# v of a linear-attention kernel: loaded six tokens per partition, cast on GpSimd, and turned twice by TensorE

## The chip, the cores and the metric

The kernel runs on one core of a Trainium2 chip. The metric is the device time of one execution in microseconds (us); less is better. Engines are named as in the profile: PE is TensorE's matmul, PEld its weight load, DVE is VectorE, ACT is ScalarE, POOL is GpSimd and SP is SyncE. "L233" is line 233 of the kernel before.

## The reference

Two stages follow each other. The first is a linear attention (RWKV-5) with B = 4, H = 8, S = 768 tokens and D = 48: a state of 48 x 48 per head decays by w and takes in one outer product per token.

```python
for t in range(S):
    kt, vt, rt = (k[:, :, t], v[:, :, t], r[:, :, t])
    cur = np.einsum('bhd,bhe->bhde', u[None] * kt, vt)
    y[:, :, t] = np.einsum('bhd,bhde->bhe', rt, state + cur)
    state = w[None, :, :, None] * state + np.einsum('bhd,bhe->bhde', kt, vt)
```

The second is a soft mixture of experts on x, which is y laid out as 3072 tokens of 384 numbers: logits = x @ phi with 32 slots (8 experts of 4 slots), a softmax over the tokens gives each slot its input, each expert is a pair of matrices (384 x 1024, relu, 1024 x 384), and a softmax over the slots mixes the slots' outputs back into the tokens. The weights w1 and w2 are 25 MB of float32 in HBM.

## The kernel before

**Tiling.** The recurrence is computed in chunks of 128 tokens. A unit m is one batch and one pair of heads (16 units, four to a batch); it has two halves of 384 tokens, three chunks each. The main loop has a step i for each of the 32 halves, from -5 on so that the pipeline fills; `mu, odd = divmod(i, 2)` gives the unit. In a step, the work of several units stands side by side: the products of unit mu + 3 (odd steps: k) and mu + 2 (even steps: r), the turns of unit mu + 2, the scores of half i + 1, the output of half i. Every instruction goes through `O(...)`, which keeps it in the order in which it is written, engine by engine. So each engine has a fixed queue, and an instruction that waits holds up all that is behind it on its engine.

**k and r.** They are loaded with six tokens to a partition (`load_kr`, L116): partition p holds tokens 6p to 6p + 5 of a head, 1152 bytes in one piece. `scale` (L228) multiplies them by powers of w and casts to bf16, on POOL for all units but the first; the factors W come from DVE (`tt`) and an exponential on ACT (`ex`), which are spread over the first steps. `t_pe` (L236) turns them on PE with six transposes, and `t_evac` (L242) copies the result out of PSUM on ACT in an order that puts token 6s + j at column 6s + j. For k, `b_pe` and `b_evac` (L249 to L257) turn that once more, to have it with the tokens of a chunk on the partitions. There are three buffers for `scale`'s result, so the product of unit m waits for the turns of unit m - 3.

**v.** It is loaded with three tokens to a partition for each half (`load_v`, L120), 576 bytes in one piece. `v_cast` (L267) makes it bf16: on POOL for unit 0, on ACT for all others, at the end of the even steps. `v_pe` (L283) puts a half in the order of tokens with nine matmuls, each of which picks a third of a chunk's tokens with a shifted selection matrix Q3, and `v_evac` (L292) copies the three chunks from the bank Vb on ACT. Each is called once in a step, for half i + 2.

**The weights and the raw buffers.** k, r and v of a batch go to one of three raw buffers; batch 3 goes to the buffer of batch 0, and its loads are issued on SP at step 3. The weights are loaded by POOL, which casts them to bf16 on the way (`load_w`, L138): w1 into a tile of its own, w2 into the raw buffers of batches 1 and 2. Their place in POOL's queue is given by a table, from step 12 on; ahead of the first stands `guard` (L576), a copy of one column of k of batch 3, which makes POOL wait until that has landed. The table's numbers are how many loads a step issues:

```python
W_AT = {12: 1, 13: 1, 14: 1, 15: 1, 17: 1, 19: 1, 20: 1, 22: 1, 23: 1, 25: 1, 26: 5}
```

**After the loop** come the last logits, then the experts: the first matrices (L628), relu, transposes (L653), the second matrices (L665, in tiles of 32 columns, one for each of four experts), and the output: a scaled matmul (L689) for each 128 tokens, and eight stores.

Of the kernel before, what the change touches and what calls it, by code (L numbers as in the profile page):

```python
# [9 lines left out]
def kernel(  # L10
# [13 lines left out]
    B, H, S, D = r.shape  # L24
    C = 128
    nC = S // C
# [7 lines left out]
    nQ = H // 2  # L34
    G = 2
    L = nC // G
    T = L * C
    P2 = 2 * D
    nN = Nn // C
    nG = B * G  # L40
    nU = B * nQ
    nH = nU * G
    J = S // C
    JV = T // C

    f32 = mybir.dt.float32
    bf = mybir.dt.bfloat16
# [4 lines left out]
    def O(ins):  # L52
        return tc.keep_in_program_order(ins)

    pe, dve, act, pool, sp = nc.tensor, nc.vector, nc.scalar, nc.gpsimd, nc.sync
# [3 lines left out]
    wk = ctx.enter_context(tc.tile_pool(name="wk", bufs=3))  # L59
# [14 lines left out]
    def raw_of(which, b):  # L74
        return raw[b % NR][:, which * RW:(which + 1) * RW]
# [3 lines left out]
    Ab = psb.tile([128, 2, 512], f32, name="Ab")  # L79
# [3 lines left out]
    Vb = psb.tile([128, 512], f32, name="Vb")  # L83
# [25 lines left out]
    O(act.dma_start(out=wu3[0:4, :, 0:D], in_=w.rearrange("(q e) d -> q e d", e=2)))  # L109
    O(act.dma_start(out=wu3[4:8, :, 0:D], in_=u.rearrange("(q e) d -> q e d", e=2)))  # L110
    O(dve.memset(warm, 0.0))
    O(dve.memset(one_f, 1.0))
    zt = cst.tile([128, nQ, 3, P2], f32, name="zt")
    O(dve.memset(zt[:], 0.0))

    def load_kr(which, src, b, h0, h1):  # L116
        O(sp.dma_start(out=raw_of(which, b).rearrange("p (h x) -> p h x", h=H)[:, h0:h1, :],
                       in_=src[b, h0:h1].rearrange("h (p j) d -> p h (j d)", j=J)))

    def load_v(b, h0, h1):  # L120
        O(sp.dma_start(out=raw_of(2, b).rearrange("p (h x) -> p h x", h=H * G)[:, h0 * G:h1 * G, :],
                       in_=v[b, h0:h1].rearrange("h (g p j) d -> p (h g) (j d)", g=G, j=JV)))

    def load_batch(b, step, h=0):
        for h0 in range(h, H, step):
# [32 lines left out]
    Q3 = cst.tile([128, QW], bf, name="Q3")  # L158
# [17 lines left out]
    ident = cst.tile([128, 128], bf, name="ident")  # L176
# [4 lines left out]
    def spread(bank, a, z):  # L181
        O(pe.matmul(bank[:, 0:z - a], one_f, w_row[:, a:z], start=True, stop=True))
        O(act.activation(out=lnw[:, a:z], in_=bank[:, 0:z - a], func=AF.Ln))
# [7 lines left out]
    def tt(j, q):  # L191
        e = (sk, sr)[j]
        O(dve.tensor_mul(W[j][:, q], lnw[:, None, q * P2:(q + 1) * P2].to_broadcast([128, J, P2]),  # L193
                         e[:, :, None].to_broadcast([128, J, P2])))

    def ex(j, q):
        O(act.activation(out=W[j][:, q], in_=W[j][:, q], func=AF.Exp))

    tt(0, 0)
    tt(1, 0)  # L200
    spread(Vb, P2, H * D)
    ex(0, 0)
    ex(1, 0)
    wT = cst.tile([128, nQ], f32, name="wT")
# [20 lines left out]
    st = {}  # L225
# [31 lines left out]
        O(dve.tensor_copy(kn[:].rearrange("p c t -> p (c t)"), T0[:, 0:S]))  # L257

    def prod_f(m):
        pr = wk.tile([128, S], bf, name="prod", bufs=2)  # L260
        st["prod", m] = pr
        O(dve.tensor_mul(pr[:].rearrange("p (s j) -> p s j", j=J),  # L262
                         T1[:, 0:S].rearrange("p (j s) -> p s j", j=J),
                         st["kT", m][:].rearrange("p (s j) -> p s j", j=J)))


    def v_cast(m):  # L267
        b, q = divmod(m, nQ)
        vb = wk.tile([128, 2, G, JV, D], bf, name="v_bf", bufs=2)
        st["vb", m] = vb  # L270
        out, src = vb[:].rearrange("p h g j d -> p (h g j d)"), raw_of(2, b)[:, 2 * q * G * JV * D:2 * (q + 1) * G * JV * D]
        if m == 0:
            O(pool.tensor_copy(out, src))
        else:
            O(act.copy(out, src))  # L275


    def at(i):
        m, g = divmod(i, G)
        b, q = divmod(m, nQ)  # L280
        return m, b, q, g, b * G + g

    def v_pe(i):  # L283
        m, b, q, g, n = at(i)
        vb = st["vb", m]
        for c in range(L):
            for j in range(JV):
                o = C * c - j + JV - 1
                O(pe.matmul(Vb[:, c * P2:(c + 1) * P2], Q3[:, o:o + C], vb[:, :, g, j, :],  # L289
                            start=(j == 0), stop=(j == JV - 1)))  # L290

    def v_evac(i):  # L292
        vn = wk.tile([128, L, 2, D], bf, name="vn", bufs=3)
        st["v", i] = vn
        O(act.copy(vn[:].rearrange("p c e d -> p (c e d)"), Vb[:, 0:L * P2]))  # L295

    def a_pe(i):
        m, b, q, g, n = at(i)
        kT, rT = st["kT", m], st["rT", m]
        for c in range(L):  # L300
            t = slice((g * L + c) * C, (g * L + c + 1) * C)
            for e in range(2):
                s = slice(64 * e, 64 * e + 64)
                O(pe.matmul(Ab[:, e, c * C:(c + 1) * C], kT[s, t], rT[s, t]))  # L304

    def mask_f(i):
        AT = wk.tile([128, 2, L, C], bf, name="AT", bufs=2)
        st["AT", i] = AT
        O(dve.tensor_mul(AT[:], Ab[:, :, 0:T].rearrange("p e (c t) -> p e c t", c=L),  # L309
                         mask_ut[:, None, None, :].to_broadcast([128, 2, L, C])))  # L310
# [123 lines left out]
    def disp_ev(n, ds_p):  # L434
        if n == 0:
            O(dve.tensor_copy(acc[:], ds_p))
        else:
            O(dve.tensor_add(acc[:], acc[:], ds_p))
# [60 lines left out]
    for i in range(-5, nH):  # L499
        mu, odd = divmod(i, 2)  # L500
        if 0 <= i + 1 < nH:
            a_pe(i + 1)
            mask_f(i + 1)
        if pend:
            disp_ev(*pend.pop())
        if i == nH - 1:
            turn(n0, (2,), Vb[:].bitcast(bf), act)
            disp(n0 - 1, ds_t)
            le_t(n0 - 1)
            let_ev(n0 - 1, None, dve)  # L510
        if 0 <= i < nH:
            y_pe(i)
            y_evac(i)
        if 0 <= i + 2 < nH:
            v_pe(i + 2)
            v_evac(i + 2)
        if 0 <= i + 1 < nH:
            m_pe(i + 1)
            z_evac(i + 1)
        if odd == 0 and 0 <= mu + 1 < nU:  # L520
            prod_f(mu + 1)
        if odd and i > 0 and mu + 2 < nU:
            b_pe(mu + 2)
            b_evac(mu + 2)
        if odd and 0 <= mu + 3 < nU:
            scale(mu + 3, 0)
        if not odd and 0 <= mu + 2 < nU:
            scale(mu + 2, 1)
        route(i, 0)
        if 0 <= mu + 2 < nU:  # L530
            t_pe(mu + 2, odd)
            route(i, 1)
            t_evac(mu + 2, odd)
            if odd and i < 0:
                b_pe(mu + 2)
                b_evac(mu + 2)
        else:
            route(i, 1)
        if odd == 0 and 0 <= mu + 2 < nU:
            v_cast(mu + 2)  # L540
        route(i, 2)
        if i == nH - 3:
            turn(n0, (0, 1), T0, act)
        if i == nH - 2:
            turn(n1, (0, 1), T1, act)
        for f, j, q in T_AT.get(i, ()):
            f(j, q)
        if i in (-4, -3):
            wu_steps(i + 4)
        if i in Z_AT:  # L550
            q = Z_AT[i]
            O(act.activation(out=zt[:, q, 2, :], in_=zt[:, q, 0, :], func=AF.Copy, scale=wT[:, q:q + 1]))
        if i == 2:
            O(pool.memset(ones[:], 1.0))
            for t in Le_t:
                O(pool.memset(t[:], 0.0))
        if i == 3:
            load_kr(0, k, B - 1, 0, H)
            load_kr(1, r, B - 1, 0, H)
            for h0 in range(0, H, 2):  # L560
                load_v(B - 1, h0, h0 + 2)
        if i == 5:
            O(act.copy(phi_b, phi_f))
        if i == 6:
            for mi in range(nM):
                for j in range(nM):
                    o = C * mi - j + nM - 1
                    O(pe.matmul(Xb[:, mi * ES:(mi + 1) * ES].rearrange("p (j g s) -> p j g s", g=2, s=Spe),
                                Q3[:, o:o + C],
                                phi_b[:, j * ES:(j + 1) * ES].rearrange("p (g j s) -> p j g s", g=2, s=Spe),  # L570
                                start=(j == 0), stop=(j == nM - 1)))
            O(act.copy(phi_s[:].rearrange("p m s -> p (m s)"), Xb[:, 0:nM * ES]))
        if i == 28:
            O(pool.memset(uns, 0.0))
        if i == min(W_AT):
            O(pool.tensor_copy(guard[:], raw_of(0, B - 1)[:, 0:1]))  # L576
        for _ in range(W_AT.get(i, 0)):
            load_w(nw)
            nw += 1
# [44 lines left out]
    for g in range(2):  # L624
        for a in range(2):
            for mi in range(nM):
                for j in range(EG):
                    O(pe.matmul(hb[g][a][32 * j:32 * j + 32, 0:FH], uns[:, mi, g, j, :],  # L628
                                w1_all[:, g * EG + j, mi, a * FH:(a + 1) * FH],
                                start=(mi == 0), stop=(mi == nM - 1), skip_group_check=True))  # L630
            src = hb[g][a][:, 0:FH].rearrange("p (q y) -> p y q", y=nF)
# [63 lines left out]
    i = 0  # L695
# [44 lines left out]
```

The softmax here doesn't subtract the row's maximum and nothing guards it: scores larger than these inputs give would overflow.

## Time and profile before

The time before is 121.42 us, the median of three runs (121.41 to 121.73). The profiled execution spans 119.7 us.

| engine | busy us | share of the span | instructions |
|---|---|---|---|
| PE | 101.7 | 85% | 1797 |
| DVE | 95.0 | 79% | 187 |
| ACT | 83.7 | 70% | 183 |
| POOL | 58.9 | 49% | 70 |

Instructions that the change touches, or that are near to those it brings:

| line, engine, what | count | mean ns of one |
|---|---|---|
| L233 POOL product of k or r | 30 | 1417 |
| L273 POOL cast of v (unit 0) | 1 | 667 |
| L275 ACT cast of v (other units) | 15 | 679 |
| L289 PE matmuls of v | 288 | 208 |
| L295 ACT copy of a half's v | 32 | 418 |
| L240 PE transposes of k and r | 192 | 225 |
| L246 ACT copy of kT, rT | 32 | 801, 804 |

The span is cut into 40 slices, and the rows of digits give each engine's busy share in tenths; one slice is 3 us. The shares are means over stages with different limits: an attention loop until about 87 us, the experts' matrices until about 103 us, the stores after it. A matmul's mean duration contains its passage through the array; what a row of matmuls costs is read from the distance between the starts of two rows in the timeline. The same goes for DVE and ACT, where an instruction begins some 0.1 us before the one ahead of it is recorded as done. In the timeline, a bracket after an instruction is the time that its engine was idle ahead of it, and what ended that. In the DMA rows, q0 is the queue of POOL's transfers and q1 that of SP's.

### The profile page before, as it was taken

The page shows a single profiled execution, that of the slowest core. Times are in us where ns is not written, and L with a number is a line of the kernel's source. Part 1 is how long each engine was busy: PE and PEld are TensorE (multiplying, and loading weights), DVE is VectorE, ACT ScalarE, POOL GpSimd, SP SyncE. Part 2 cuts the span into 40 slices and gives each one's busy share as a digit, 9 for nine tenths or more (in the row PEclk, how much of TensorE's full clock was granted, in tenths as well). Part 3 has the DMA queues.
Part 4 walks back from the last instruction along what each step waited for, and adds up shares of the span by engine and source line. Part 5 has one row for each costly group of instructions (what it writes and reads, how often), then busy time and mean ns, then how long its engine had stood idle before and what let it go on. Part 6 is the DMA issues. An engine that isn't in the chain of part 4 may idle for free.

```text
span 119.7 us, 4336 instructions
## 1 busy us (share of the span) xinstructions
PE 101.7 (85%) x1797; PEld 81.9 (68%) x1797; DVE 95.0 (79%) x187; ACT 83.7 (70%) x183; POOL 58.9 (49%) x70
## 2 busy tenths in 40 slices
PE   5897877799999999999999999999979996795000
PEld 1456766578988888898888888888866686682000
DVE  6889999999999999899999899999943510499000
ACT  4259987898979988888898988998964510398000
POOL 7326744699999999796877591111000000011100
PEclk9999999999999999999999999999999999999855
DMA  3999999999999999999999999999999997179991
GB/s 89 365 344 372 377 370 370 333 393 358 320 384 381 342 219 224 211 220 207 223 207 225 207 218 214 214 215 218 215 216 211 218 203 146 17 288 386 427 407 70
DMA packets 20797, 31.79 MB, mean 266 GB/s; under 512 B 1129, under 2 KB 17898, under 8 KB 20650
## 3 DMA queue, kind: packets, MB, share of 16 engines
q0 software_dynamic: 2960, 15.34, 57.1%
q1 hardware_dynamic: 17648, 16.03, 39.7%
q8 instruction: 14, 0.23, 0.7%
q10 hardware_dynamic: 170, 0.15, 0.4%
q14 instruction: 5, 0.04, 0.1%
HBM read 39.38 MB, written 4.72 MB: 368 GB/s over the span
## 4 chain that ended last, share of the span: by engine, by line
PE 39%; DMA 23%; DVE 20%; ACT 6%; issue 4%; POOLq 0%; DVEq 0%; ACTq 0%
DMA raw<-in_moe_w_dram 21%; PE Vb L289 5%; PE T L240 5%; PE Ab L304 4%; PE Yb L357 4%; DVE prod L262 3%; DVE W L193 3%; DVE AT L309 3%; PE Mb L330 3%; PE T L252 3%; DVE raw L691 2%; PE Yb L370 2%; DMA LexpT<-in_w_dram 2%; ACT rT L246 2%; PE Xb L392 2%
## 5 line engine op out<-in xcount | busy, mean ns | idle before, releaser
L233 POOL TENSOR_TENSOR kr<-raw,W 128x576 bf16<-128x576 f32 x30 | 42.0, 1417 | 13.6 <-PE T L240 5.1
L309 DVE TENSOR_TENSOR AT<-Ab,mask_ut 128x768 bf16<-128x768 f32 x32 | 30.4, 949 | 0.8 <-PE Ab L304 0.6
L289 PE MATMUL Vb<-v_bf,Q 128*128 128x96 bf16 x288 | 17.8, 208 | 0.3 <-ACT vn L295 0.3
L289 PEld LDWEIGHTS <-Q 128*128 128x128 bf16 x288 | 16.1, 99 | 1.7 <-issue 0.3
L240 PE MATMUL T<-ident,kr 128*128 128x128 bf16 x192 | 16.6, 225 | 0.7 <-POOL kr L233 0.7
L246 ACT COPY kT<-T 128x768 bf16<-128x768 bf16 x16 | 12.8, 801 | 4.4 <-PE T L240 3.2
L246 ACT COPY rT<-T 128x768 bf16<-128x768 bf16 x16 | 12.9, 804 | 3.4 <-PE T L240 2.8
L262 DVE TENSOR_TENSOR prod<-T,kT 128x768 bf16<-128x768 bf16 x16 | 15.2, 950 | 0.0
L347 DVE TENSOR_TENSOR dv<-vn,Mb 128x288 bf16<-128x288 bf16 x32 | 14.2, 443 | 0.0
L295 ACT CAST vn<-Vb 128x288 bf16<-128x288 f32 x32 | 13.4, 418 | 0.1
L346 DVE TENSOR_TENSOR Z<-Mb,zt 128x288 bf16<-128x288 f32 (+1 forms) x32 | 12.8, 400 | 0.7
L240 PEld LDWEIGHTS <-kr 128*128 128x128 bf16 x192 | 12.2, 100 | 1.5 <-POOL kr L233 0.8
L377 ACT CAST x<-Yb 128x288 bf16<-128x288 f32 x32 | 13.1, 409 | 0.1
L709 POOL DMA_DIRECT2D out_dram<-W x1 | 0.6, 552 | 24.7 <-DVE W L691 24.7
L304 PE MATMUL Ab<-rT,kT 64*128 64x128 bf16 x192 | 10.9, 219 | 2.0 <-DVE AT L309 2.0
L330 PE MATMUL Mb<-vn,kn 128*128 128x96 bf16 (+2 forms) x80 | 11.2, 238 | 0.0
L357 PE MATMUL Yb<-vn,AT 128*128 128x48 bf16 x192 | 10.3, 185 | 0.1
L275 ACT CAST v_bf<-raw 128x576 bf16<-128x576 f32 x15 | 10.2, 679 | 0.0
L143 POOL DMA_DIRECT2D raw<-in_moe_w_dram x10 | 5.5, 558 | 7.9 <-DMA raw<-in_moe_w_dram 2.9
L357 PEld LDWEIGHTS <-AT 128*128 128x128 bf16 x192 | 7.1, 96 | 3.3
L304 PEld LDWEIGHTS <-kT 64*128 64x128 bf16 x192 | 5.5, 94 | 5.5 <-DVE AT L309 1.9
L370 PE MATMUL Yb<-dv,ident 128*128 128x288 bf16 x32 | 9.1, 284 | 0.2
(143 smaller groups left out, 220.2 us busy)
## 6 DMA issues: line engine op xcount, KB each, us to landing
w_all<-in_moe_w_dram POOLq DMA_DIRECT2D x8, 768.0 KB, 13.6
raw<-in_moe_w_dram POOLq DMA_DIRECT2D x7, 768.0 KB, 18.9
raw<-in_v_dram SPq DMA_DIRECT2D x12, 288.0 KB, 7.2
raw<-in_r_dram SPq DMA_DIRECT2D x8, 288.0 KB, 5.2
raw<-in_k_dram SPq DMA_DIRECT2D x2, 1152.0 KB, 9.9
raw<-in_r_dram SPq DMA_DIRECT2D x2, 1152.0 KB, 9.3
raw<-in_k_dram SPq DMA_DIRECT2D x7, 288.0 KB, 6.0
out_dram<-raw POOLq DMA_DIRECT2D x1, 1536.0 KB, 6.7
```

The source lines that it names most:

```text
L233: O(eng.tensor_mul(kr[:, j].rearrange("p j (h s) -> p j h s", s=64)[:, :, :, 0:D], src, W[j][:, q].rearrange("p j (h d) -> p j h d", h=2)))
L240: O(pe.transpose(bank[:, x * C:(x + 1) * C], kr[:, j, x, :], ident[:]))
L246: O(act.copy(t[:].rearrange("p (s j) -> p s j", j=J), bank[:, 0:S].rearrange("p (j s) -> p s j", j=J)))
L262: O(dve.tensor_mul(pr[:].rearrange("p (s j) -> p s j", j=J), T1[:, 0:S].rearrange("p (j s) -> p s j", j=J), st["kT", m][:].rearrange("p (s ...
L289: O(pe.matmul(Vb[:, c * P2:(c + 1) * P2], Q3[:, o:o + C], vb[:, :, g, j, :], start=(j == 0), stop=(j == JV - 1)))
L295: O(act.copy(vn[:].rearrange("p c e d -> p (c e d)"), Vb[:, 0:L * P2]))
L304: O(pe.matmul(Ab[:, e, c * C:(c + 1) * C], kT[s, t], rT[s, t]))
L309: O(dve.tensor_mul(AT[:], Ab[:, :, 0:T].rearrange("p e (c t) -> p e c t", c=L), mask_ut[:, None, None, :].to_broadcast([128, 2, L, C])))
L330: O(pe.matmul(o, kn[:, g * L + c, :], vc, start=first, stop=True, skip_group_check=True))
L347: O(dve.tensor_mul(dv[:], st["v", i][:].rearrange("p c e d -> p (c e) d"), Mb[:, 288:288 + 2 * L, None].to_broadcast([128, L * 2, D])))
L357: O(pe.matmul(Yb[:, o:o + D], AT[:, e, c, :], vn[:, c, e, :], start=first, stop=False, skip_group_check=True))
L377: O(act.copy(st["x", n][:, :, q * P2:(q + 1) * P2], Yb[:, 0:L * P2].rearrange("p (c e) -> p c e", c=L)))
```

## The change

v is loaded like k and r, six tokens to a partition and 1152 bytes in one piece. Its cast goes to POOL for all units but 1 to 3, which ACT casts, and stands at the end of the odd steps, for unit mu + 3. Selection by matmul is replaced by two turns, a whole unit at a time. At the even steps `vt_pe` turns the two heads of unit mu + 2 with twelve transposes into the partitions 0 to 47 and 64 to 111 of bank Vb, and `vt_evac` copies them out in the order of tokens. At the odd steps `vn_pe` turns the six chunks back, into the same bank, and `vn_evac` copies them out on ACT. The purpose is that one layout and one load function serve all three inputs, and that v is read from HBM in longer pieces. Rows 48 to 63 of Vb are never written by a turn but are read, so the bank is cleared once at the start. The first logarithm's second matmul moves to another bank; `prod`, `v_bf` and `vT` have one buffer each.

```diff
+    O(dve.memset(Vb[:], 0.0))
...
     def load_v(b, h0, h1):
-        O(sp.dma_start(out=raw_of(2, b).rearrange("p (h x) -> p h x", h=H * G)[:, h0 * G:h1 * G, :],
-                       in_=v[b, h0:h1].rearrange("h (g p j) d -> p (h g) (j d)", g=G, j=JV)))
+        load_kr(2, v, b, h0, h1)
...
-    spread(Vb, P2, H * D)
+    spread(Ab[:, 0, :], P2, H * D)
...
-        pr = wk.tile([128, S], bf, name="prod", bufs=2)
+        pr = wk.tile([128, S], bf, name="prod", bufs=1)
...
     def v_cast(m):
-        vb = wk.tile([128, 2, G, JV, D], bf, name="v_bf", bufs=2)
+        vb = wk.tile([128, 2, J, D], bf, name="v_bf", bufs=1)
...
-        if m == 0:
-            O(pool.tensor_copy(out, src))
-        else:
-            O(act.copy(out, src))
+        if 0 < m < nQ:
+            O(act.copy(out, src))
+        else:
+            O(pool.tensor_copy(out, src))
+
+    def vt_pe(m):
+        vb = st["vb", m]
+        for j in range(J):
+            for e in range(2):
+                O(pe.transpose(Vh[64 * e:64 * e + D, j * C:(j + 1) * C], vb[:, e, j, :], ident[:]))
+
+    def vt_evac(m):
+        vT = wk.tile([128, S], bf, name="vT", bufs=1)
+        st["vT", m] = vT
+        O(act.copy(vT[0:PV].rearrange("p (s j) -> p s j", j=J),
+                   Vh[0:PV, 0:S].rearrange("p (j s) -> p s j", j=J)))
+
+    def vn_pe(m):
+        vT = st["vT", m]
+        for c in range(nC):
+            O(pe.transpose(Vh[:, c * C:c * C + PV], vT[0:PV, c * C:(c + 1) * C], ident[0:PV, 0:PV]))
+
+    def vn_evac(m):
+        vn = wk.tile([128, nC, 2, D], bf, name="vn", bufs=3)
...
+        O(act.copy(vn[:].rearrange("p c e d -> p (c e) d"),
+                   Vh[:, 0:S].rearrange("p (x s) -> p x s", s=64)[:, :, 0:D]))
...
-        if 0 <= i + 2 < nH:
-            v_pe(i + 2)
-            v_evac(i + 2)
+        if 0 <= mu + 2 < nU:
+            if odd:
+                vn_pe(mu + 2)
+                vn_evac(mu + 2)
+            else:
+                vt_pe(mu + 2)
+                vt_evac(mu + 2)
...
-        if odd == 0 and 0 <= mu + 2 < nU:
-            v_cast(mu + 2)
+        if odd and 0 <= mu + 3 < nU:
+            v_cast(mu + 3)
```

More of the change, by code (lines that the diff above doesn't have):

```diff
@@ L264, in prod_f @@
                          st["kT", m][:].rearrange("p (s j) -> p s j", j=J)))
+    Vh = Vb[:].bitcast(bf)
+    PV = 64 + D
     def v_cast(m):
         b, q = divmod(m, nQ)
-        vb = wk.tile([128, 2, G, JV, D], bf, name="v_bf", bufs=2)
+        vb = wk.tile([128, 2, J, D], bf, name="v_bf", bufs=1)
         st["vb", m] = vb
-        out, src = vb[:].rearrange("p h g j d -> p (h g j d)"), raw_of(2, b)[:, 2 * q * G * JV * D:2 * (q + 1) * G * JV * D]
-        if m == 0:
+        out, src = vb[:].rearrange("p h j d -> p (h j d)"), raw_of(2, b)[:, 2 * q * J * D:2 * (q + 1) * J * D]
+        if 0 < m < nQ:
+            O(act.copy(out, src))
+        else:
             O(pool.tensor_copy(out, src))
-        else:
-            O(act.copy(out, src))
+    def vt_pe(m):
[14 more added lines that the diff above has]
+        vn = wk.tile([128, nC, 2, D], bf, name="vn", bufs=3)
+        for g in range(G):
+            st["v", m * G + g] = vn[:, g * L:(g + 1) * L]
+        O(act.copy(vn[:].rearrange("p c e d -> p (c e) d"),
+                   Vh[:, 0:S].rearrange("p (x s) -> p x s", s=64)[:, :, 0:D]))
     def at(i):
@@ L281, in at @@
         return m, b, q, g, b * G + g
[L283 to L295, printed above, removed]
     def a_pe(i):
```

## The prediction

> **What bounds the kernel now.** I read the page first, then the chain and the waits, then the timeline of POOL, then the DMA queues in stretches of 1 us.
>
> ```profile
> DMA  3999999999999999999999999999999997179991
> ...
> DMA raw<-in_moe_w_dram 21%; PE Vb L289 5%; PE T L240 5%; PE Ab L304 4%; PE Yb L357 4%; DVE prod L262 3%; DVE W L193 3%; DVE AT L309 3%; PE Mb L330 3%; PE T L252 3%; DVE raw L691 2%; PE Yb L370 2%; DMA LexpT<-in_w_dram 2%; ACT rT L246 2%; PE Xb L392 2%
> ...
> ACT W L677 <- PE Yb L665: 7.3, 1, 7.3
> PE Xb L665 <- DMA raw<-in_moe_w_dram: 1.5, 3, 0.5
> ```
>
> The DMA engines are full in every slice but the first until slice 33 (about 99 us), and the chain holds one long piece that is no engine's: the weights, from 77.77 to 102.52 us. The second matmuls (L665) stop for their last pieces (at 99.26, 101.15, 102.52), while ACT has had nothing to do for 7.3 us. So the end is the end of the weight transfer at 102.5 us, plus a tail of 119.7 - 102.5 = 17.2 us that the change doesn't touch. The attention loop ends near 87 us, and PE has done all that needs no late weights at 98.7: it has about 0.6 us to spare before the first of these waits. The weight stream runs at a constant 215 GB/s from 42 us on, so it ends early or late as it starts early or late. Who starts it? POOL, in program order:
>
> ```profile
> 22.06 1.42 POOL L233 TENSOR_TENSOR kr<-raw,W 128x576 bf16<-128x576 f32 x1 [1.41 <-ACT W L197]
> 23.41 0.21 POOL L554 MEMSET ones<- 128x128 bf16 x1
> 23.55 0.79 POOL L556 MEMSET Le<- 128x384 bf16 x2
> 24.30 13.72 POOL L233 TENSOR_TENSOR kr<-raw,W 128x576 bf16<-128x576 f32 x10
> 37.95 0.20 POOL L576 COPY guard<-raw 128x1 f32<-128x1 f32 x1
> 38.07 0.75 POOL L140 DMA_DIRECT2D w_all<-in_moe_w_dram  x1
> ```
>
> From 24.30 to the guard there is no bracket: ten products back to back (1.37 us from one start to the next), no wait. POOL is the bound of this stretch, though the page gives it 49% of the span. The DMA queues show what hangs on it (share of 16 engines in the microseconds from 36, 39, 40 and 41):
>
> ```profile
> q1 hardware_dynamic: 344, 0.39, 109.1%
> ...
> q1 hardware_dynamic: 605, 0.34, 108.6%
> ...
> q0 software_dynamic: 1, 0.01, 3.0%
> ...
> q0 software_dynamic: 21, 0.13, 62.1%
> q1 hardware_dynamic: 330, 0.18, 59.6%
> ```
>
> q1 carries r, k, v, q0 the weights. The first weight packet moves just before 41 us, 2.9 us after its issue at 38.07, and q1 runs dry near 41.6. The hand-over is just in time: counting the share that q0 had already, the weights start in effect at 41.3 and need 61.2 us. Any lateness of POOL there is a hole in the DMA.
>
> **What the Trainium skill says.** "GPSIMD Engine Reference", 4.1 Engine selection: elementwise work with one input runs near line rate on GpSimd, with two about twice as slow as VectorE. The trace agrees on the ratio: its one cast (L273) took 0.67 us, a product of the same 576 columns 1.42. "DMA: Bandwidth & Descriptors", Why small descriptors are slow: a fixed cost per packet; the trace shows 0.34 MB/us for v alone (576-byte packets, from 39 us) and 0.39 for k and r (1152 bytes, from 36 us). The same page, Latency and other measured facts, gives about 1 us to the first byte of a GpSimd transfer; here 2.9 us pass, and I use those. "TensorEngine Tiling (Array Packing)", Key Properties: tiles of the array work at the same time, but a change of mode drains it. The trace has the first half: at L665 four tiles of 32 columns with 192 moving columns each take 0.09 us together.
>
> **The change part by part.**
>
> *DMA of v.* v is 4.72 MB. At 0.34 MB/us it takes 13.9 us, at 0.39 12.1. The gain is 1.5 to 1.8 us; q1 would run dry near 40.0.
>
> *POOL.* Casts 4 to 15 move from ACT to POOL. In the queue the casts of units 4, 5, 6, 7 and 8 (steps 3, 5, 7, 9, 11) stand between the memsets and the guard. Each takes 0.67 us, 0.62 as one of a row: 5 x 0.62 = 3.1 us, and there is no idle time to take them in. Behind them stand the guard, all weight issues and the later products. A cast also waits now for vt_pe of the unit before, since v_bf has one buffer. For unit 8 that is PE's step 10, which has its v work at 38.7 us before; POOL reaches this cast, by its own pace alone, about 40.5, so the wait is short or none. Afterwards POOL needs 2 x 1.37 + 0.62 + 0.6 for each issue, 4.0 to 4.6 us a unit, against PE's 4.4: the next weights come in time, the second with little to spare.
>
> *ACT.* A unit had two vn casts (418 ns) and a v cast (679), 1.52 us. It gets a vT copy (as kT, L246: 801) and a vn copy of 576 columns (between the 384-column copy of xT, 0.48, and 801: 0.64), 1.44. From unit 4 on nothing changes. At the start it does: by the last exponential that POOL's products wait for (step 1, run at 21.30), ACT had four vn casts and two v casts; now it has three vT copies, three vn copies and three v casts. From start to start (0.29, 0.58; 0.70, 0.55, 0.58) that is 5.5 us instead of 2.3, 3.2 more. ACT's idle time between 8 and 22 us is 3.1 us, but much of it is waiting for DVE, which itself has almost none from 12 us on:
>
> ```profile
> 18.48 0.69 ACT L197 ACTIVATE W<-W 128x576 f32<-128x576 f32 x1 [0.22 <-DVE W L193]
> 21.30 0.68 ACT L197 ACTIVATE W<-W 128x576 f32<-128x576 f32 x1 [0.84 <-DVE W L193]
> ```
>
> The added work comes ahead of kT, rT and the exponentials in ACT's queue, kT delays kn on DVE, and DVE's next W product delays the next exponential. PE adds to it: vt_pe of unit 0 stands ahead of the first t_pe, when six transposes still take 0.75 us. So the startup slips by something between 0.3 us (all of it in gaps) and 3.2 (none). I take 1.8: following the queues step by step puts kT of unit 1 later by about 2 us, and I hold part of that back. POOL's product at 22.06 waits for exactly this exponential, so its row of products starts 1.8 us later.
>
> *PE.* Before, a unit had 18 matmuls of 96 columns in 2 x 0.38 us. Now it has 12 turns with 48 columns of weights and 128 moving, and 6 of 112. One at a time they cost what t_pe does (0.34 us for six): 0.68 + 0.33 = 1.01 us, 0.25 more. Two at a time in tiles 64 wide: 0.34 + 0.33, 0.09 less. DVE needs 4.4 us a unit in any case, so a saving is worth nothing. I take half, +0.1 us a unit, 1.5 us by the loop's end; with the startup it ends some 3 us later, and PE is ready for the late weights near 102.
>
> *Edits at nothing.* The memset of Vb (about 0.5 us on DVE by the 1.02 us of zt, 2.25 times its size) goes into the 0.55 us in which DVE waits for the first logarithm. One buffer for prod and vT: their next writers come after their last readers have been waited for by the same engine. The logarithm's spread uses another bank.
>
> *Sum.* The first weight is issued 1.8 + 3.1 = 4.9 us later, at 43.0; its first packet moves at 45.9; the DMA is empty from 40.0 to then, so v's shorter transfer buys nothing. The weights end 61.2 us later, at 107.1, against 102.5: +4.6. PE's 102 lies below that. The time is 121.4 + 4.6 = 126.0.
>
> **The rivals.**
> 1. *Only the casts count* (startup slip 0.3, casts 3.1): the weights start 3.4 us later, less the 0.35 us of overlap lost anyway: 121.4 + 3.05 = 124.5. For it: ACT's 3.1 us of gaps. Against: they lie elsewhere than the added work.
> 2. *The transfer decides* and POOL keeps its date: 1.5 us less of DMA, 119.9, faster. For it: the DMA row at 9 throughout and the gap between 0.34 and 0.39. Against: the stretch from 24.30 to 37.95 without a wait.
> 3. *The compute loop becomes the bound*: turns one at a time, drains between tile modes, and the two hops over ACT (vT, then vn in the same bank) that PE waits for with everything queued behind, 0.2 to 0.3 us a step over 32 steps, 6 to 9 us: 128.5 to 131. For it: PE at 9 in the slices and ACT at 2.76 of 3. Against: ACT has a step of about 2.2 us for each hop.
> 4. *No change*: slip and gain cancel, 121.4. Nothing in the profile sets them equal.
>
> **How the numbers follow.** The forecast with slips of 1 to 3 us has 0.70, rival 1 0.12, rival 2 0.06, rival 3 0.10, rival 4 0.02. Faster 0.06, same 0.03, slower 0.91. The bounds of the startup (0.3 to 3.2) give 124.5 to 127.4; a cast cheaper or a first packet sooner takes off 0.7, and weights that come late once or twice add about 1. The range is 123.7 to 128.6, which leaves out rivals 2 and 4 and most of 3.
>
> **What would show it.** Right: the GB/s row has a hole of 5 to 6 us between about 40 and 46 us where before it had none; POOL shows guard and first weight near 43 with five casts in an unbroken row ahead of them; the weights still take 61 us; the end moves with them. The startup slip is read from the start of POOL's row of products (24.30 before). Wrong: the first weight before 41 us (rival 1 or 2); PE waiting for ACT vT or vn in each step, or L665 with no wait for weights (rival 3); a DMA row with no hole. What I see least well is the startup.

## The result, and the profile after

The changed kernel takes 128.12 us (median of four runs, 127.91 to 128.35), the kernel before 121.52 in the same session. The ratio is 1.054, 95% interval 1.052 to 1.057: 6.6 us slower. The forecast was 126.0 (123.7 to 128.6), slower.

The page of the changed kernel, slices of 3.2 us (digits are tenths; GB/s is what the DMA moved), and its chain:

```profile
PEclk9999657999999999999999999999999997699955
DMA  4999999999999008999999999999999999259991
GB/s 110 332 279 362 388 390 381 388 391 386 387 391 320 20 5 158 217 217 208 213 218 213 214 217 210 217 215 224 208 210 219 212 214 194 40 194 382 410 434 74
...
DMA raw<-in_moe_w_dram 19%; DVE AT L322 10%; DVE prod L262 6%; DVE dv L360 5%; POOL kr L233 4%; DVE kn L257 3%; POOL raw L143 2%; PE Xb L682 2%; PE Yb L682 2%; DVE Z L359 1%; PE Vb L284 1%; POOL v_bf L278 1%; PE T L706 1%; PE T L240 1%; PE T L252 1%
```

Where the DMA row held 9 throughout, it now has two zeros, about 41 to 47.5 us. After the hole the weights move at 215 GB/s as before. The chain ends in the weights again, and POOL, absent from it before, is now part of it (its pieces there lie between 73.9 and 82.0 us, at the last issues, not at the guard).

POOL's queue in the changed kernel, the columns being start, duration, instruction and, in brackets, idle time before it:

```profile
25.86 1.41 POOL L233 TENSOR_TENSOR kr<-raw,W 128x576 bf16<-128x576 f32 x1 [1.41 <-ACT W L197]
...
28.09 1.41 POOL L233 TENSOR_TENSOR kr<-raw,W 128x576 bf16<-128x576 f32 x1
29.44 0.67 POOL L278 CAST v_bf<-raw 128x576 bf16<-128x576 f32 x1
30.06 2.78 POOL L233 TENSOR_TENSOR kr<-raw,W 128x576 bf16<-128x576 f32 x2
...
44.04 0.66 POOL L278 CAST v_bf<-raw 128x576 bf16<-128x576 f32 x1 [1.05 <-issue]
44.66 1.41 POOL L233 TENSOR_TENSOR kr<-raw,W 128x576 bf16<-128x576 f32 x1
46.02 0.19 POOL L593 COPY guard<-raw 128x1 f32<-128x1 f32 x1
46.14 0.75 POOL L140 DMA_DIRECT2D w_all<-in_moe_w_dram  x1
```

The exponential that ran at 21.30 now runs at 25.11, and with it ends POOL's wait at 25.86; the row of products starts at 28.09 instead of 24.30 (+3.8), and takes 17.9 us to the guard instead of 13.7 (+4.3: a wait of 1.05 and 3.2 of casts). So the first weight is issued at 46.14 instead of 38.07. Its first packet moves between 47.5 and 47.6, 1.4 us later; before it took 2.8. The stream starts 6.7 us later than before (40.85) and is used up 6.6 us later: DVE's first work with the product of the last weights comes at 109.95 instead of 103.30 (the first line is from the kernel before, the second from the changed one). That is the whole loss.

```profile
103.30 0.42 DVE L676 TENSOR_SCALAR W<-Xb,csr 128x192 bf16<-128x192 f32 x1 [7.06 <-PE Xb L665]
...
109.95 0.42 DVE L693 TENSOR_SCALAR W<-Xb,csr 128x192 bf16<-128x192 f32 x1 [9.55 <-PE Xb L682]
```

The waits at the end of the changed kernel (total, times, longest):

```profile
ACT W L694 <- PE Yb L682: 9.8, 1, 9.8
DVE W L693 <- PE Xb L682: 9.6, 1, 9.6
...
PE Xb L682 <- DMA raw<-in_moe_w_dram: 3.0, 2, 2.6
```

PE waits longer for the weights than before (3.0 us against 1.5), though the loop ends later too: the first filler matmul after it (L149) starts at 93.52 us in place of 89.36.

### The profile page after: what moved, and what is told of

Same layout as the page of the kernel before. It is cut to its first block, busy times and chain, and to the rows that moved or that the text cites. A ratio compares the mean times of both kernels' runs of the same rounds, so it can differ in the third digit from the quotient of the medians.

```text
span 126.4 us, 4298 instructions
## 1 busy us (share of the span) xinstructions
PE 104.2 (82%) x1795; PEld 81.6 (65%) x1797; DVE 95.4 (76%) x188; ACT 86.9 (69%) x171; POOL 66.9 (53%) x82
## 4 chain that ended last, share of the span: by engine, by line
DVE 27%; DMA 19%; PE 12%; POOL 8%; issue 6%; POOLq 0%
DMA raw<-in_moe_w_dram 19%; DVE AT L322 10%; DVE prod L262 6%; DVE dv L360 5%; POOL kr L233 4%; DVE kn L257 3%; POOL raw L143 2%; PE Xb L682 2%; PE Yb L682 2%; DVE Z L359 1%; PE Vb L284 1%; POOL v_bf L278 1%; PE T L706 1%; PE T L240 1%; PE T L252 1%
## 5 line engine op out<-in xcount | busy, mean ns | idle before, releaser
L233 POOL TENSOR_TENSOR kr<-raw,W 128x576 bf16<-128x576 f32 x30 | 42.0, 1413 | 12.4 <-ACT W L197 8.2
L240 PE MATMUL T<-ident,kr 128*128 128x128 bf16 x192 | 17.1, 230 | 0.0
L289 ACT COPY vT<-Vb 112x768 bf16<-112x768 bf16 x16 | 13.0, 810 | 2.5 <-PE Vb L284 2.2
L240 PEld LDWEIGHTS <-kr 128*128 128x128 bf16 x192 | 12.7, 103 | 0.3 <-issue 0.2
L278 POOL CAST v_bf<-raw 128x576 bf16<-128x576 f32 x13 | 9.2, 707 | 5.9 <-issue 2.3
L284 PE MATMUL Vb<-ident,v_bf 128*48 128x128 bf16 x192 | 8.9, 233 | 3.3 <-ACT v_bf L276 2.7
L343 PE MATMUL Mb<-vn,kn 128*128 128x96 bf16 (+2 forms) x80 | 11.7, 245 | 0.0
L284 PEld LDWEIGHTS <-v_bf 128*48 128x48 bf16 x192 | 6.1, 108 | 7.6 <-ACT v_bf L276 3.7
L301 ACT COPY vn<-Vb 128x576 bf16<-128x576 bf16 x16 | 10.7, 666 | 0.1
L682 PE MATMUL Xb<-raw,W 128*32 128x192 bf16 x64 | 7.0, 267 | 3.0 <-DMA raw<-in_moe_w_dram 3.0
L257 DVE COPY kn<-T 128x768 bf16<-128x768 bf16 x16 | 8.8, 551 | 0.6 <-PE T L252 0.5
```

Source lines behind the costliest of these rows:

```text
L233: O(eng.tensor_mul(kr[:, j].rearrange("p j (h s) -> p j h s", s=64)[:, :, :, 0:D], src, W[j][:, q].rearrange("p j (h d) -> p j h d", h=2)))
L240: O(pe.transpose(bank[:, x * C:(x + 1) * C], kr[:, j, x, :], ident[:]))
L284: O(pe.transpose(Vh[64 * e:64 * e + D, j * C:(j + 1) * C], vb[:, e, j, :], ident[:]))
L289: O(act.copy(vT[0:PV].rearrange("p (s j) -> p s j", j=J), Vh[0:PV, 0:S].rearrange("p (j s) -> p s j", j=J)))
L682: O(pe.matmul(SO[x][32 * j:32 * j + 32, :], hT[g][:, y, 32 * j:32 * j + 32], w2_of(g * EG + j)[:, y, x * HD:(x + 1) * HD], start=(g == 0 a ...
```

## The experiments

Each was timed against the kernel before on the same chip. Its times varied more in these later sessions than in the first (121.4 to 123.1), so the ratios with their intervals are what to compare; each line gives the median of before of its session.

**The weights late, all else as before.** The kernel before, with another table:

```diff
-    W_AT = {12: 1, 13: 1, 14: 1, 15: 1, 17: 1, 19: 1, 20: 1, 22: 1, 23: 1, 25: 1, 26: 5}
+    W_AT = {17: 1, 18: 1, 19: 1, 20: 1, 21: 1, 22: 1, 23: 1, 24: 1, 25: 1, 26: 6}
```

> The kernel before, with nothing changed but the steps at which POOL issues the weights: the first at step 17 instead of 12, so at about 46 us. My theory (the weights' start sets the end): the weights end as much later as they start, first packet near 47.7, 127.5 to 128.5 us, the whole loss of the change without one of its edits to v. Rival (the added work on PE, ACT and POOL slows the loop, and the weights only follow it): no work is added here, 121.4 to 122.5 us.

Measured: 130.62 us (before 122.2), ratio 1.071, 1.066 to 1.076. Slower than expected, because the issue came later than I had aimed for; 1.3 us of that is a later startup in the profiled execution (POOL's row starts at 25.58, not 24.30, with the same instructions up to there):

```profile
48.10 0.18 POOL L576 COPY guard<-raw 128x1 f32<-128x1 f32 x1
49.23 0.75 POOL L140 DMA_DIRECT2D w_all<-in_moe_w_dram  x1 [0.94 <-issue]
```

The first packet moves at 50.7, 9.8 us later than in the kernel before, and DVE's first work with the product of the last weights starts at 112.36, 9.1 us later. With no work of v changed, a late start alone costs more than the whole change (it is also later, 9.8 against 6.7 us). The rival of the added work doesn't explain this run.

**The weights early, v as changed.**

```diff
-    W_AT = {12: 1, 13: 1, 14: 1, 15: 1, 17: 1, 19: 1, 20: 1, 22: 1, 23: 1, 25: 1, 26: 5}
+    W_AT = {8: 1, 9: 1, 10: 1, 11: 1, 13: 1, 15: 1, 17: 1, 20: 1, 22: 1, 23: 1, 25: 1, 26: 4}
```

> The changed kernel, with the first weights issued four steps earlier (8, 9, 10, 11, ... instead of 12, 13, 14, 15, ...), so the first at about 38.3 us; all work on v as changed. My theory: the hole in the DMA closes, the weights end near 101 us, and what is left of the loss is the compute loop alone, which ends 4 us later than in the kernel before: 122.5 to 124.5 us. Rival (the loop is the bound): 127 to 128 us.

Measured: 123.88 us (before 122.2), ratio 1.015, 1.009 to 1.021. Within my theory's range: the table alone gives back 4 to 5 of the 6.6 us (by the medians, by the ratios). But not all that is left is the loop: I had spread the later weights too thin, the stream ran at 185 GB/s in place of 215 between 60 and 80 us, and PE still waited once for the last weights, for 0.83 us.

**Five casts left out.**

```diff
     def v_cast(m):
...
+        if 4 <= m <= 8:
+            st["vb", m] = st["vb", 3]
+            return
```

> The changed kernel without the casts of units 4 to 8, the five ahead of the guard on POOL; these units are given unit 3's v, so that part of the output is of other data, with all other work in place. My theory: the guard comes 4.3 us earlier (five casts of 0.65 and the wait of 1.05 us), near 41.8, and the time is 123.5 to 124.5 us. Rival (PE's turns and ACT's copies are the cost): 127.5 to 128.5 us.

Measured: 126.96 us (before 122.2), ratio 1.041, 1.036 to 1.046. The guard came at 41.79, as expected, but only about a third of the gain arrived. POOL in this run:

```profile
41.79 0.21 POOL L596 COPY guard<-raw 128x1 f32<-128x1 f32 x1
41.91 0.75 POOL L140 DMA_DIRECT2D w_all<-in_moe_w_dram  x1
42.68 1.42 POOL L233 TENSOR_TENSOR kr<-raw,W 128x576 bf16<-128x576 f32 x1
47.87 0.66 POOL L281 CAST v_bf<-raw 128x576 bf16<-128x576 f32 x1 [3.77 <-PE Vb L287]
48.48 0.59 POOL L140 DMA_DIRECT2D w_all<-in_moe_w_dram  x1
```

The next cast, that of unit 9, waits 3.77 us for PE's turns out of the one buffer, and the second weight stands behind it. The first is finished by then: from 48 to 49 us q0 moves eight packets and next to no bytes. So the expectation missed the single buffer, and the run shows what I had put at "short or none": a cast that waits holds up the weights behind it.

**The other casts on POOL as well.**

```diff
-        if 0 < m < nQ:
-            O(act.copy(out, src))
-        else:
-            O(pool.tensor_copy(out, src))
+        O(pool.tensor_copy(out, src))
```

> The changed kernel with the casts of units 1 to 3 on POOL too, as all others. It tests the startup slip, which I put down to the added work in ACT's queue ahead of the exponentials. If ACT's queue is the cause, its first steps get 1.7 us shorter, POOL's row of products starts 1 to 2 us earlier than 28.1, and the time is 126 to 127.2 us. If the slip comes from PE (turns in its queue, each waiting for the one before), the row starts as late as now and the time stays at 128.

Measured: 127.71 us (before 122.2; 126.99 to 128.20), ratio 1.045, 1.038 to 1.053. POOL's row starts at 27.48, 0.6 us earlier (0.4 to 0.7 against the four profiles that leave the startup as changed, 27.85 to 28.14); the guard comes at 46.30, no earlier. So ACT's casts are a small part of the slip. That part of my theory, as I had weighed it, fell.

That the guard gained nothing has a reason that I had overlooked. With one buffer, the cast of unit 8 can't start before PE has turned unit 7 out of it, and it starts 0.65 us after that turn does, 2 us ahead of the guard: turn, cast and guard at 43.39, 44.04 and 46.02 in the changed kernel, at 43.67, 44.32 and 46.30 here, and at 41.05, 41.70 and 43.67 in the run below with the turns moved. In all three the guard's date is set by PE, not by POOL's row. The turn in the changed kernel (before, PE's work on v in that step starts at 38.72):

```profile
43.39 0.52 PE L284 MATMUL Vb<-ident,v_bf 128*48 128x128 bf16 x12
```

For the slip, PE's timeline in the changed kernel gives another reason:

```profile
12.75 0.52 PE L284 MATMUL Vb<-ident,v_bf 128*48 128x128 bf16 x12 [1.80 <-ACT v_bf L276]
13.20 0.51 PE L240 MATMUL T<-ident,kr 128*128 128x128 bf16 x6
13.64 0.40 PE L317 MATMUL Ab<-rT,kT 64*128 64x128 bf16 x6
14.86 0.74 PE L295 MATMUL Vb<-ident,vT 112*128 112x112 bf16 x6 [0.81 <-ACT vT L289]
15.39 0.69 PE L343 MATMUL Mb<-vn,kn 128*128 128x288 bf16 x3
15.88 0.26 PE L347 MATMUL Mb<-ucol,prod 128*128 128x2 bf16 x3
16.00 0.80 PE L240 MATMUL T<-ident,kr 128*128 128x128 bf16 x6
```

The turns wait (for a cast, then for the copy vT), and with them everything behind: the turns of k, then the state products L343, whose results DVE wants. And the PEclk row above has 6, 5, 7 in the slices from 13 to 22 us: after this idle time the granted clock is 0.50 from about 13.8 to 20.6 us, and six transposes take 0.80 us (L240 at 16.00) where they take 0.50 from 22 us on, at 1.00.

**The turns behind the others, up to step 0.** `v_turn` holds the lines that are taken out.

```diff
-        if 0 <= mu + 2 < nU:
-            if odd:
-                vn_pe(mu + 2)
-                vn_evac(mu + 2)
-            else:
-                vt_pe(mu + 2)
-                vt_evac(mu + 2)
+        if i >= 1:
+            v_turn(mu, odd)
...
+        if i < 1:
+            v_turn(mu, odd)
         if odd and 0 <= mu + 3 < nU:
             v_cast(mu + 3)
```

> The changed kernel with v's turns and copies at the end of the steps up to step 0, behind t_pe and b_pe on PE and behind kT and rT on ACT; from step 1 on as changed. It tests the startup slip: moving the casts off ACT left PE idle for 2 us all the same, so I now put the slip down to the turns standing ahead of the others in PE's fixed queue. If so, POOL's row of products starts 1.5 to 3 us earlier than 28.1, the guard with it, and the time is 125.5 to 126.8 us. If the slip is the amount of work on ACT (3.2 us more), the row starts within 0.7 us of 28.1 and the time stays above 127.3.

Measured: 125.73 us (before 121.83), ratio 1.032, 1.029 to 1.034. Inside the expectation. The clock and POOL's row in this run:

```profile
PEclk9999999999999999999999999999999999999655
```

```profile
25.75 1.41 POOL L233 TENSOR_TENSOR kr<-raw,W 128x576 bf16<-128x576 f32 x1
...
43.67 0.19 POOL L599 COPY guard<-raw 128x1 f32<-128x1 f32 x1
```

2.3 of the 3.8 us of the slip are gone, and the time falls by 2.4 (by the ratios 2.8). The amount of work on every engine is the same. Whether the stalls or the low clock weigh more within the 2.3 us, this run can't say: it removed both. In the last run below, with the turns moved too, the clock did fall to 0.50 for about 3.4 us, and POOL's row started at 25.91 all the same; but that run has other casts on POOL, so the two stay unseparated.

**Two buffers for v_bf.**

```diff
-        vb = wk.tile([128, 2, J, D], bf, name="v_bf", bufs=1)
+        vb = wk.tile([128, 2, J, D], bf, name="v_bf", bufs=2)
...
-        vn = wk.tile([128, nC, 2, D], bf, name="vn", bufs=3)
+        vn = wk.tile([128, nC, 2, D], bf, name="vn", bufs=2)
```

> The changed kernel with two buffers for v_bf (and two instead of three for vn, to make room), so that a cast no longer waits for the turns of the unit before. My theory: the wait of 1.05 us ahead of unit 8's cast goes, the guard comes near 45.0 instead of 46.0 us, and the time falls by about 1 us to 127.0. If that wait is nothing (the cast waited for something else), the time stays at 128.

Measured: 126.86 us (before 121.83), ratio 1.041, 1.038 to 1.043. As expected. The bracket ahead of unit 8's cast is gone and the guard comes at 44.71, 1.3 us earlier. POOL's row now takes 16.7 us to the guard, 3.05 more than before: the casts alone.

```profile
42.74 0.67 POOL L278 CAST v_bf<-raw 128x576 bf16<-128x576 f32 x1
43.36 1.41 POOL L233 TENSOR_TENSOR kr<-raw,W 128x576 bf16<-128x576 f32 x1
44.71 0.19 POOL L593 COPY guard<-raw 128x1 f32<-128x1 f32 x1
```

In the changed kernel the profile puts the 1.05 us down to "issue"; that it was the buffer is shown only by taking the single buffer away.

**The layout of v alone, in the kernel before.**

```diff
     def load_v(b, h0, h1):
-        O(sp.dma_start(out=raw_of(2, b).rearrange("p (h x) -> p h x", h=H * G)[:, h0 * G:h1 * G, :],
-                       in_=v[b, h0:h1].rearrange("h (g p j) d -> p (h g) (j d)", g=G, j=JV)))
+        load_kr(2, v, b, h0, h1)
```

> The kernel before with one edit: v loaded six tokens to a partition (1152 bytes in a piece). The rest takes the numbers as if they lay as before, so v's tokens are in a wrong order; all work is the same. My theory: SP's loads end 1.5 to 1.8 us earlier, near 40.0, but the weights start when POOL issues them, so that only the overlap of 0.3 us is won: 121.0 to 121.5 us. Rival (the bytes moved set the end): 119.7 to 120.2 us.

Measured: 121.24 us (before 121.83; 120.15 to 121.77), ratio 0.994, 0.990 to 0.997. A gain of 0.8 us, give or take 0.4. That leaves room for the upper part of the expected gain (up to 0.5); the full 1.5 us lies outside.

**The same, and the weights one step earlier.**

```diff
-    W_AT = {12: 1, 13: 1, 14: 1, 15: 1, 17: 1, 19: 1, 20: 1, 22: 1, 23: 1, 25: 1, 26: 5}
+    W_AT = {11: 1, 12: 1, 13: 1, 14: 1, 16: 1, 18: 1, 20: 1, 22: 1, 23: 1, 25: 1, 26: 5}
```

> As the run with the layout of v alone in the kernel before (v's tokens in a wrong order), and the first weights one step earlier, at about 36.7 us. My theory: now the shorter transfer can be used, the weights start in effect 1.5 us earlier, and so does the end, as far as PE allows, which had 0.6 us to spare ahead of its first late weights and more behind: 119.8 to 120.8 us. Rival (POOL's date is no limit): the same as with the layout alone.

Measured: 120.79 us (before 121.83), ratio 0.992, 0.989 to 0.995. Inside the expectation, but its interval overlaps that of the layout alone: that the earlier issue added to the gain is not shown. Nor was the earlier table run without the new layout, so of the 1 us that the two are worth together, only the 0.8 of the run above belongs to the layout alone.

**Three mends together**: the later turns and two buffers, by the edits above, and the weights from step 8 on, the later ones closer than in the early run.

```diff
-    W_AT = {12: 1, 13: 1, 14: 1, 15: 1, 17: 1, 19: 1, 20: 1, 22: 1, 23: 1, 25: 1, 26: 5}
+    W_AT = {8: 1, 9: 1, 10: 1, 11: 1, 13: 1, 15: 1, 16: 1, 18: 1, 20: 1, 22: 1, 24: 1, 26: 4}
```

> The changed kernel with three mends together: v's turns behind the others up to step 0, two buffers for v_bf, and the first weights from step 8 on, with the later ones spread so that the stream does not run dry. My theory: no hole is left in the DMA, the weights end near 101.5 us or before, and the loop, which ends some 2 us later than in the kernel before, becomes the bound by about 0.5 to 1 us: 121.5 to 122.8 us, near the kernel before but not below it. If the hole was all of the loss and the loop is free, 119.8 to 120.5 us.

Measured: 121.50 us (before 121.82, twenty runs against thirty), ratio 0.997, 0.995 to 0.999. **And with all casts on POOL:**

> As the run with the three mends, and the casts of units 1 to 3 on POOL too. If ACT's queue still holds up the first steps, the loop ends up to 1 us earlier: 120.8 to 122. If not, the same as with three mends, 121.5 to 122.8 us.

Measured: 121.20 us (before 121.82), ratio 0.995, 0.992 to 0.997. All 6.6 us are back, and the kernel is a little faster than before, by 0.3 to 1.0 us. The kernel before was not given an earlier table for comparison. Three mends end at the low edge of what I expected of them, and I had not expected them below the kernel before; the casts on POOL are within their expectation, but the two intervals overlap, so that they added anything is not shown. The page of the last kernel:

```profile
DMA  3999999999999999999999999999999993079991
```

The hole is gone, the weights' last packets come about 1.4 us earlier than in the kernel before (101.4 against 102.8), and PE waits for none of them. DVE's first work with their product starts at 103.10, against 103.30 before. The chain that ended last no longer holds the weights: the loop, which ends 2 us later than before (L149 at 91.34), has taken the place of the transfer as the bound.

## Why the prediction was right

**The sum.** The measured 128.12 lies near the upper edge of the range (128.6), and that it lies inside is in part luck: the startup slip and the buffer were set too low by about 3 us together, and an error the other way, in the first packet, took 1.5 back. With the time of the first packet as I had it, I estimate from these figures some 129.6 us, outside the range.

**What bounds the kernel.** Right, and shown from both sides: late weights alone cost 8.4 us in the kernel before, early weights alone give back 4 to 5 of 6.6 in the changed one. The weight stream kept its length, so the time went with its start.

**The hole in the DMA.** Right in kind and place. Forecast from 40.0 to 45.9 us; found from about 41 to 47.5.

**Casts.** 3.1 us forecast; 3.2 in POOL's row, and 3.05 where two buffers leave the casts alone. With one buffer they were not what set the guard's date; the next point is. The ratio that I had checked on the trace, cast to product on POOL, is not the one of POOL to VectorE; a product takes 1.42 us on POOL and 0.75 to 0.89 on DVE (L233), 1.6 to 1.9 times as long.

**The wait for the one buffer.** "Short or none" was wrong: 1.05 us on POOL, and 1.3 at the guard with two buffers. I had timed PE's side with the kernel before, without the slip of PE itself. PE's turn of unit 7 starts at 43.39, 4.7 us later than PE's work at 38.7 that I had taken, while POOL alone would have reached the cast of unit 8 near 43.0, 2.5 us later than my 40.5. So PE came last, and the startup slip reached the guard by way of PE and the buffer as well as by POOL's row.

**The startup slip.** The worst-sized term: 1.8 us taken, 3.2 as the upper bound, 3.8 found. The step that failed is that the slip is ACT's added work less ACT's gaps. Moving ACT's casts away gave back 0.6 us. Moving the turns in PE's queue gave back 2.3 with no work removed: an order of instructions, with the low clock that followed PE's idle time. I had seen the turns of unit 0 ahead of t_pe, but not those of unit 1, which wait for a cast that is itself behind two copies.

The 3.8 itself rests on one profile of the kernel before, and its startup is not steady. Four profiles have its startup code, two of them with the new layout of v: POOL's row starts at 24.30 and 24.18 in two, and at 25.58 and 25.53 in the others, where one small product on DVE (ucol, L214) took 1.35 and 1.40 us in place of 0.16; why is open. With the turns moved, the row starts at 25.75 to 25.91 in three profiles. So the last 1.5 us of the slip, which no run separated, shrink to 0.2 to 0.4 against the later of these starts.

**From issue to first packet.** 2.9 us used as a fixed time, 1.4 found, which took back the 1.5 us named above. It is no fixed time: while SP's loads fill the DMA, the first packet comes about when they begin to ebb (figures in the last section). So "any lateness of POOL there is a hole" was too strict: by these figures, an estimate, POOL could have come some 1.4 us later in the kernel before without moving the first packet.

**PE in the loop.** Taken at +0.1 us a unit; it is about nothing. In the changed kernel's timeline the two kinds of turns and what follows them:

```profile
38.95 0.52 PE L284 MATMUL Vb<-ident,v_bf 128*48 128x128 bf16 x12
39.40 0.26 PE L332 MATMUL Mb<-Z,ident 128*128 128x192 bf16 x1
...
40.98 0.46 PE L295 MATMUL Vb<-ident,vT 112*128 112x112 bf16 x6
41.27 0.41 PE L343 MATMUL Mb<-vn,kn 128*128 128x288 bf16 x3
```

Start to start, 0.45 + 0.29 = 0.74 us, against 0.76 for the selection before. Twelve turns of 48 columns in 0.45 us are 37 ns each, between one at a time (57) and two at a time (28), as the Trainium skill ("TensorEngine Tiling (Array Packing)", Key Properties), by which tiles can work in parallel, lets one expect in part: the turns gain something here, not the full factor of two. That the gain comes from tiles running together is inferred and not tested. The other reading, that 48 columns of weights load sooner, has little for it: the selections before, with 128 columns of weights and 96 moving, took 0.38 / 9 = 42 ns each, so the time went by the moving columns. The loop ends 4.2 us later, not 3, nearly all of it from the startup; PE still waits for the weights after it.

**The rivals.** The first (casts only) fails on the startup. The second (the transfer decides) fails on the hole, though its gain is real with the weights in time: 0.8 us in the kernel before. The third (the loop becomes the bound) is not the case in the changed kernel, but it is in the mended one.

## What to carry to other kernels

An engine that is half idle over the span can still be full in the stretch that leads up to an issue of its own; ask what is queued behind each instruction that you put there, and whether it waits. When a transfer that sets the end is started by such a queue, its start is part of the path, and while that start is late, a shorter transfer ahead of it buys nothing. A single buffer between two queues ties their dates together: look which side reaches it last in the new kernel, not in the old one. In fixed queues, place new work that waits behind the work that others wait for, most of all while the pipeline fills.

## What the runs showed of the hardware

From the issue of the first weight on POOL to its first packet it took 1.4 to 1.5 us where SP's loads had ended or were far down: in the changed kernel, with the weights late, with five casts left out, with all casts on POOL, with the turns moved, with two buffers and with the layout alone. Where SP's loads still filled the DMA, the date of the issue hardly counted: in the four runs with the long pieces of v and an early issue (early weights, layout with the earlier table, and the two with three mends), issues at 37.99, 36.58, 36.04 and 36.06 had their first packets at 39.5, 39.3, 39.4 and 39.1, when the share of SP's queue began to fall below 100%. In the kernel before it took 2.8 us.

PE's granted clock fell to 0.50 in all six profiles in which PE was idle for 1.60 to 2.17 us between 10 and 13 us, and in none of the six in which that gap was 0.61 to 1.55 us. It stayed there for 6.6 to 6.9 us in five of the six, and about 3.4 us in the run with three mends and all casts on POOL, which has the turns moved too. In the changed kernel six transposes took 0.80 us in that stretch, instead of 0.50. The recorded clock doesn't tell all: the first six transposes, near 8 us, took 0.78 to 0.85 us in eleven of the twelve profiles at a recorded 1.00.
